# Asking for the first attention unit's keys and query at other places of the projection stage

## The chip, the cores and the metric

The kernel runs on one core of a Trainium2 chip. The metric is the device time of one execution in microseconds (us); of several runs the median is given.

## The reference

Two independent layers work on inputs of 2048 positions and 448 channels, and their outputs are joined along the last axis.

```python
# layer A: a diagonal state-space convolution
K = 2.0 * einsum("dn,dnl->dl", C, exp((A * dt[:, None])[:, :, None] * pos)).real
y = irfft(rfft(u_t, 2 * L) * rfft(K, 2 * L))[:, :, :L] ; y = y + u * D_skip
# layer B: attention with 16 heads of 28 channels
q, k, v = split(x @ wqkv)
p = softmax(einsum("bhqd,bhkd->bhqk", q, k) * scale)
b = einsum("bhqk,bhkd->bhqd", p, v) @ wo
return concatenate([a, b], axis=-1)
```

All arithmetic is float32 or close to it: the queries and keys are kept as a high and a low part, stacked in rows of 32 partitions.

## The kernel before

**Units of attention.** The 16 heads are four groups (`G`) of four heads (`HG`), the 2048 queries are four chunks of 512 (`CQ`). A unit is one group and one chunk; the units 0 to 15 are worked off in that order. For each unit three tensors lie in on-chip memory: the stacked keys `khat` of the group (one 128 x 2048 slab per head j, of four transfers of 256 KB), the stacked queries `qhat` (four transfers of 256 KB) and the key differences `kdif` of the group (for each head four transfers of 64 KB). `load_k(g, j, pool)`, `load_q(u, rows)` and `load_kd(g, j, rows)` ask for them. They are read from DRAM buffers that the projection has written (`k<-hl`, `q<-hl` and `kd<-dhl` in the profile).

**The first stage** does two things side by side until unit 0 can start. TensorE projects x into q, k and v: a list `work` of 48 jobs, for each of the four chunks c the k and q of groups 0 to 3 and four blocks of v; in the last chunk the four v blocks come first, so the last eight jobs are k0, q0, k1, q1, k2, q2, k3, q3. A job is issued by `project()`, and the evacuation of the job *before* it follows: ScalarE and VectorE write the high and low halves into a tile `hl`, which has two buffers, and one transfer of 512 KB takes it to DRAM. Beside that, `seeds(o)` for o = 0 to 7 prepares layer A on VectorE, ScalarE and GpSimd, in 13 steps each, and writes two tiles to DRAM (`sd<-sg`, step 11, and `sd<-qhat`, step 12). The second one is built in a `qhat` buffer: `places` (step 8) takes it with two GpSimd memsets. There are three `qhat` buffers, shared by the seeds and by the queries of the units.

**The order** is written out in slots t = 0 to 40. Step i of `seeds(o)` lies in slot 4o + i. In each slot the projection advances to 48(t+1)/37 jobs, then the seeds' steps follow, then what `ahead` holds for the slot:

```python
A0, A1, KW = 26, 34, (33, 35, 36)
ahead = collections.defaultdict(list)
for i in range(2 * HG):
    ahead[A0 + i].append(lambda i=i: load_kd(0, i // 2, range(2 * (i % 2), 2 * (i % 2) + 2)))
for i in range(2):
    ahead[A1 + i].append(lambda i=i: load_q(0, range(2 * i, 2 * i + 2)))
for j, t in enumerate(KW):
    ahead[t].append(lambda j=j: load_k(0, j, k0_p))
...
for t in range(n_stage):
    while work and n_work - len(work) < n_work * (t + 1) / PW:   # PW = 37
        project()
    for f in slots[t] + ahead.get(t, []):
        f()
```

After slot 36 the last evacuation, the fourth head's keys (`load_k(0, 3)`), the query of unit 1 and the v tiles of group 0 are asked for. In this stage the order of the program is a priority for the scheduler and not a fixed order (`KEPT["p"]` is empty); all transfers are issued from one engine, SyncE, whose queue (SPq) is worked in order. The slab of head j in `khat` of group 0 also holds the projection weights of group j until the last q and k of that group have been projected, so its load waits for TensorE.

**The maxima of unit 0** come behind the slots: for each of 16 pairs (head, block of 128 queries), four matmuls of 512 keys. The first uses `kdif` and goes through ScalarE (`rl`, Relu), VectorE joins it to the second, and reduces the third and the fourth (`mx`). Their end is `m<-mx`, a transposition, and the start of the attention loop, in which every engine's order is fixed.

In the profile nearly every instruction carries the line of one helper, L75, so groups are told apart by the names of the tiles.

Of the kernel before, what the change touches and what calls it, by code (L numbers as in the profile page):

```python
# [40 lines left out]
PS = 1  # L41
SGB, XB, XL = 2, 5, 4
K0, KP, KD, UP = 0, 3.5, 4, 3
A0, A1, KW = 26, 34, (33, 35, 36)

N1 = 32
N2 = 64
# [43 lines left out]
def body(ctx, tc, a, out):  # L91
# [5 lines left out]
    def pool(stack, name, bufs=1, space=None, side=None):  # L97
        kw = {} if space is None else {"space": space}
        if side:
            kw["side"] = side  # L100
        return stack.enter_context(tc.tile_pool(name=name, bufs=bufs, reuse_waits="tile", **kw))
# [31 lines left out]
    k0_p = pool(k0_st, "k0_p", side="right")  # L133
# [11 lines left out]
    def load_k(g, j, p):  # L145
        if j == 0:
            t = k0_t if g == 0 else p.tile([128, HG, L], F32R, name="khat")
            kt_g[g] = [t[:, i] for i in range(HG)]
        for r in range(4):
            nc.sync.dma_start(kt_g[g][j][32 * r:32 * r + 32, :].bitcast(F32), k_d[g][r % 2, 32 * j:32 * j + 32, :])  # L150
# [3 lines left out]
    def load_v(g, c):  # L154
        v_g[g, c] = t = v_p.tile([128, NK // NQ, HG, 32], F32, name="v", bufs=5)
        nc.sync.dma_start(t.rearrange("p t h e -> p t (h e)"), v_d[c][:, g])
# [8 lines left out]
    def load_q(u, rows=range(4)):  # L165
        g, c = divmod(u, NQ)
        if 0 in rows:
            q_u[u] = q_p.tile([128, HG, CQ], F32R, name="qhat", bufs=3)
        t = q_u[u]
        for r in rows:  # L170
            nc.sync.dma_start(t[32 * r:32 * r + 32].bitcast(F32), q_d[g][c][r // 2].rearrange("(j p) q -> p j q", j=HG))
# [40 lines left out]
    with ExitStack() as st:  # L212
# [47 lines left out]
        t = a["A_log_dt"]  # L260
# [252 lines left out]
        ahead = collections.defaultdict(list)  # L513
# [2 lines left out]
        for i in range(2):  # L516
            ahead[A1 + i].append(lambda i=i: load_q(0, range(2 * i, 2 * i + 2)))

        for j, t in enumerate(KW):
            ahead[t].append(lambda j=j: load_k(0, j, k0_p))  # L520

        def project():

            e = work.pop(0)() if work else None
            while pend:
                pend.pop(0)()
            if e:
                pend.append(e)

        for t in range(n_stage):  # L530
            while work and n_work - len(work) < n_work * (t + 1) / PW:
                project()
            for f in slots[t] + ahead.get(t, []):
                f()
            if t + 1 == PW:
                project()
                wst.close()
                load_k(0, HG - 1, k0_p)
                load_q(1)
                for c in range(NQ):  # L540
                    load_v(0, c)
# [581 lines left out]
```

## Time and profile before

| | us |
|---|---|
| median of three runs (1330.11 to 1336.95) | 1332.18 |
| the profiled execution, device time | 1331.76 |
| its span in the profile | 1329.9 |

| engine | busy us | share of the span |
|---|---|---|
| TensorE, matmul (PE) | 1235.2 | 93% |
| VectorE (DVE) | 990.1 | 74% |
| ScalarE (ACT) | 953.2 | 72% |
| GpSimd (POOL) | 838.4 | 63% |

The attention loop starts near 260 us, and from there TensorE is busy in nearly all of its time. The shares above are averages over the first stage and the loop. All times below are counted from the start of the span. The 1.9 us between the span and the device time lie outside the profile.

### The profile page before, as it was taken

To read this page: it belongs to the slowest core of one execution; us is meant where nothing else is said; L and a number is where in the kernel's file an instruction comes from. 1 tells how busy PE (TensorE), PEld (TensorE's weight loads), DVE (VectorE), ACT (ScalarE), POOL (GpSimd) and SP (SyncE) were. 2 spreads that over 40 slices of the span, in tenths; PEclk is the share of its full clock that TensorE was granted. 3 is DMA by queue.
4 is the path that set the end of the run, shared out by engine and by line. 5 is a ranking of instruction groups with operands and counts; after the bars stand their busy time and mean duration, and the time that the engine had idled before them with its cause. 6 is when DMAs were issued, how large, how long until landed. Compare 5 with 4: busy or idle time off the path is not lost.

```text
span 1329.9 us, 33195 instructions
## 1 busy us (share of the span) xinstructions
PE 1235.2 (93%) x12625; PEld 705.0 (53%) x12625; DVE 990.1 (74%) x2138; ACT 953.2 (72%) x2067; POOL 838.4 (63%) x704
## 2 busy tenths in 40 slices
PE   6878885699999999999999999999999999898997
PEld 5656763355555555555555555555555545444433
DVE  5897786787777887787788988888886858757311
ACT  4876762388888888888888888888886656555553
POOL 2686681378788788888779999989992202211211
PEclk9989888799999999999999999999999999999999
DMA  6677669725856546468634233732415553825485
GB/s 188 207 272 264 217 211 287 206 57 122 191 134 152 128 129 163 135 165 235 172 95 95 61 72 89 165 78 69 100 50 148 192 157 134 263 102 162 150 217 140
DMA packets 200088, 205.36 MB, mean 154 GB/s; under 512 B 95992, under 2 KB 158520, under 8 KB 197880
## 3 DMA queue, kind: packets, MB, share of 16 engines
q1 hardware_dynamic: 199928, 203.23, 55.1%
q8 instruction: 100, 1.64, 0.5%
q14 instruction: 60, 0.49, 0.1%
HBM read 120.73 MB, written 82.18 MB: 153 GB/s over the span
## 4 chain that ended last, share of the span: by engine, by line
PE 69%; DVE 14%; DMA 5%; ACT 5%; POOL 4%; issue 2%; SPq 1%; ACTq 0%; POOLq 0%; DVEq 0%
PE pm L75 39%; PE pss L75 15%; PE po L75 15%; DVE mx L75 2%; DVE p L75 2%; DVE tri L75 2%; DVE pr L75 1%; POOL qhat L75 1%; ACT p L75 1%; DVE rl L75 1%; DVE sg L75 1%; DVE qhat L75 1%; ACT tri L75 1%; DMA qhat<-q 1%; DVE px L75 1%
## 5 line engine op out<-in xcount | busy, mean ns | idle before, releaser
L75 ACT ACTIVATE p<-pss 128x512 f32<-128x512 f32 x1024 | 561.6, 611 | 118.7 <-PE pss L75 114.3
L75 PE MATMUL pss<-qhat,khat 128*128 128x512 f32 x1024 | 403.3, 400 | 3.8 <-ACT p L75 3.7
L75 DVE TENSOR_REDUCE mx<-pm 128x1 f32<-128x512 f32 x500 | 321.5, 684 | 102.4 <-PE pm L75 100.9
L75 PE MATMUL pm<-khat,qhat 128*128 128x512 f32 x749 | 326.9, 439 | 19.3 <-DVE mx L75 6.7
L75 POOL TENSOR_TENSOR e<-e,sdb 128x256 f32<-128x256 f32 x168 | 201.8, 1201 | 126.7 <-ACT e L75 107.8
L75 PE MATMUL po<-p,v 128*32 128x512 f32 x2048 | 269.9, 596 | 0.0
L75 POOL TENSOR_TENSOR e<-e,eu 128x256 f32<-128x256 f32 x168 | 248.1, 1477 | 13.2
L75 PEld LDWEIGHTS pm<-khat,qhat 128*128 128x128 f32 x749 | 141.5, 189 | 215.1 <-ACT p L75 47.0
L75 DVE CUSTOM_DVE_ANT_0 rl<-pm,rl 128x512 f32<-128x512 f32 x249 | 171.5, 689 | 66.0 <-ACT rl L75 62.2
L75 PEld LDWEIGHTS pss<-qhat,khat 128*128 128x128 f32 x1024 | 190.6, 188 | 50.8 <-ACT p L75 12.4
L75 POOL TENSOR_TENSOR eu<-e,sdb 128x256 f32<-128x256 f32 x168 | 202.0, 1202 | 0.0
L75 POOL TENSOR_TENSOR p<-pr,pr 64x448 f32<-64x448 f32 x32 | 40.9, 1278 | 197.3 <-DVE pr L75 186.3
L75 DVE TENSOR_TENSOR g<-g,zg 128x128 f32<-128x128 f32 x392 | 162.1, 414 | 4.0 <-ACT zg L75 0.6
L75 ACT ACTIVATE rl<-pm 128x512 f32<-128x512 f32 x249 | 151.1, 607 | 16.8 <-PE pm L75 16.8
L75 PE MATMUL pm<-xh,khat 112*128 112x512 f32 x256 | 92.3, 444 | 21.3 <-DVE hl L75 9.8
L75 PE MATMUL pm<-kdif,qhat 128*128 128x512 f32 x249 | 100.9, 405 | 2.3 <-DVE mx L75 1.3
L75 DVE TENSOR_TENSOR zg<-g,zg 128x128 f32<-128x128 f32 x224 | 87.9, 392 | 5.1
L75 PEld LDWEIGHTS pm<-e,g 128*32 128x32 f32 x3584 | 57.6, 110 | 44.0 <-issue 17.8
L75 PE MATMUL pm<-e,g 128*32 128x64 f32 x3584 | 73.7, 222 | 1.9 <-POOL e L75 1.9
L75 ACT ACTIVATE y<-pm 128x448 f32<-128x448 f32 x48 | 26.3, 549 | 65.9 <-issue 32.8
L75 PEld LDWEIGHTS pm<-xh,khat 112*128 112x128 f32 x256 | 53.4, 213 | 36.6 <-DVE hl L75 11.2
L75 PEld LDWEIGHTS po<-p,v 128*32 128x32 f32 x2048 | 55.8, 110 | 22.4 <-issue 17.9
(134 smaller groups left out, 1503.9 us busy)
## 6 DMA issues: line engine op xcount, KB each, us to landing
sdb<-sd SPq DMA_DIRECT2D x56, 336.0 KB
khat<-k SPq DMA_DIRECT2D x64, 256.0 KB
qhat<-q SPq DMA_DIRECT2D x64, 256.0 KB
sd<-sg SPq DMA_DIRECT2D x8, 1456.0 KB
k<-hl SPq DMA_DIRECT2D x16, 512.0 KB
q<-hl SPq DMA_DIRECT2D x16, 512.0 KB
mw<-in_mw SPq DMA_DIRECT2D x16, 512.0 KB
sd<-qhat SPq DMA_DIRECT2D x8, 896.0 KB
```

What stands on the lines that cost most here:

```text
L75: i = f(*args, **kw)
```

## The change

The eight requests for parts of `kdif` move from the slots 26 to 33 to the slots 16 to 23. The two requests for the halves of the first query `qhat` move from the slots 34 and 35 to 24 and 25. The keys of heads 0, 1 and 2 keep their slots 33, 35 and 36, but stand at the head of the slot, before its projection and its seeds' steps; until now they stood at its end. Nothing is computed differently, and the number of instructions and transfers stays the same.

```diff
-A0, A1, KW = 26, 34, (33, 35, 36)
+A0, A1, KW = 16, 24, (33, 35, 36)
...
-        for j, t in enumerate(KW):
-            ahead[t].append(lambda j=j: load_k(0, j, k0_p))
+        firsts = {t: lambda j=j: load_k(0, j, k0_p) for j, t in enumerate(KW)}
...
         for t in range(n_stage):
+            if t in firsts:
+                firsts[t]()
             while work and n_work - len(work) < n_work * (t + 1) / PW:
                 project()
             for f in slots[t] + ahead.get(t, []):
```

## Prediction

> **What bounds the kernel now.** I read the page first, for the size of the stage that the change touches.
>
> ```profile
> PE   6878885699999999999999999999999999898997
> ```
>
> One digit is 33 us. From the ninth on TensorE is at 9 nearly throughout: that is the attention loop, which the change does not enter. What it can save or lose lies in the first eight digits and shifts all that follows. In them I read the chain that ended last, to find where the stage passes from projection to attention.
>
> ```profile
> 203.16 11.80 DMA qhat<-q
> 214.96 0.14 issue
> 215.10 0.78 PE pt L75
> 215.90 0.61 ACT rl L75
> 216.53 0.69 DVE rl L75
> ...
> 247.47 0.21 DVE m L75
> ```
>
> The columns are start, duration and what ran. For 11.8 us the chain is one transfer, the second half of unit 0's query; the maxima begin when it has landed. On VectorE they last from 216.53 to 247.47, 30.9 us. Next I read the timelines of SyncE's queue, ScalarE, VectorE and TensorE around that wait, to see what is late once the query is not.
>
> ```profile
> 184.39 1.24 SPq L75 DMA_DIRECT2D sd<-qhat  x1
> 185.68 2.55 SPq L75 DMA_DIRECT2D kdif<-kd  x2
> 188.33 1.20 SPq L75 DMA_DIRECT2D k<-hl  x1
> 194.90 0.38 SPq L75 DMA_DIRECT2D q<-hl  x1
> 195.32 1.32 SPq L75 DMA_DIRECT2D kdif<-kd  x2
> 196.75 1.75 SPq L75 DMA_DIRECT2D khat<-k  x4
> 198.96 0.39 SPq L75 DMA_DIRECT2D k<-hl  x1
> 199.40 1.69 SPq L75 DMA_DIRECT2D qhat<-q  x2
> 201.19 0.42 SPq L75 DMA_DIRECT2D q<-hl  x1
> 201.65 0.58 SPq L75 DMA_DIRECT2D sd<-sg  x1
> ```
>
> ```profile
> 205.16 0.69 ACT L75 ACTIVATE hl<-pm,kones 128x512 fp32r<-128x512 f32 x1 [6.68 <-DMA k<-hl]
> ```
>
> ```profile
> 205.88 0.75 DVE L75 SCALAR_TENSOR_TENSOR hl<-pm,kones,hl 128x512 fp32r<-128x512 f32 x1 [4.26 <-ACT hl L75]
> ...
> 210.94 0.69 DVE L75 TENSOR_TENSOR hl<-pm,hl 128x512 fp32r<-128x512 f32 x1 [1.05 <-ACT hl L75]
> ```
>
> ```profile
> 203.21 0.40 PE L75 MATMUL pm<-xl,khat 112*128 112x512 f32 x1
> ```
>
> Four things are to be seen. In this stretch SyncE's queue stands in the order of the program: slot 33 gives k<-hl (188.33, job k1) and q<-hl (194.90, q1), then its requests; slot 34 k2 (198.96), slot 35 q2 (201.19). TensorE ends the last projection, q3, near 203.6 and then waits. The evacuation of k3 (ScalarE 205.16) waits 6.68 us for k2's transfer, whose buffer it takes: issued at 198.96, that lands near 205.1, 6.2 us later, behind the first head's four key transfers of 196.75. And VectorE finishes the last evacuation, q3, at 211.63 (210.94 + 0.69), so today's wait for the query hides a second one that ends only 4.9 us before 216.53.
>
> **The change, part by part.** The sizes that pass through the queue:
>
> ```profile
> khat<-k SPq DMA_DIRECT2D x64, 256.0 KB
> sd<-sg SPq DMA_DIRECT2D x8, 1456.0 KB
> k<-hl SPq DMA_DIRECT2D x16, 512.0 KB
> ...
> sd<-qhat SPq DMA_DIRECT2D x8, 896.0 KB
> ```
>
> ```profile
> 120.00:125.00 5.00, 5.00 (x27) 3.84 (x27) 3.32 (x5) 1.66 (x3) 2.25 (x1) 1.00 1.05 385
> 190.00:195.00 5.00, 2.33 (x11) 1.58 (x9) 3.88 (x6) 4.06 (x6) 2.76 (x2) 0.94 0.48 176
> 200.00:205.00 5.00, 3.61 (x13) 2.54 (x12) 1.51 (x5) 0.00 (x0) 4.40 (x5) 0.88 0.97 263
> ```
>
> The last two columns are the DMA engines' busy share and GB/s: full engines move 0.26 (200 to 205) to 0.38 MB per us (120 to 125); I take 0.30, nearer the row of this stretch.
>
> *The query leaves.* Four transfers, two at 199.40 and two behind the sd<-sg of 201.65, go to the slots 24 and 25. The 11.8 us wait goes entirely. Next late is the evacuation chain above, not TensorE.
>
> *The first head's keys rise* in the queue from 196.75 to about 186, behind sd<-qhat and ahead of k1 (188.33). They need k0's transfer and q0's matmuls, both past. Their 1.05 MB need 3.5 us; between 190 and 195 the engines were half idle (0.48), and the kdif pairs that stood here are gone, so k1 and q1, which follow, land in time for their buffers. Cost: nothing; without that cover, up to 3.5 us on the evacuation of k2, which takes k1's buffer.
>
> *k2's transfer* then has no keys ahead of it. Its time lies between 6.2 us (as now) and that of a transfer with an empty queue; the nearest row for the latter is q1's on the chain:
>
> ```profile
> 194.90 2.87 DMA q<-hl
> ```
>
> I take 2.9, because the keys of head 1 stand behind k2 (slot 35) and no longer head 0's ahead of it. It lands near 201.9 instead of 205.1, and k3's evacuation on ScalarE and VectorE runs 3.2 us sooner. The Trainium skill, page DMA: Bandwidth & Descriptors, section Anatomy of one DMA, fits a transfer at about 2.0 us plus its bytes at 436 GB/s, on the GpSimd path; for 512 KB that estimates 3.2 us, and the sum below would be 1325.1. It is measured on another issuing path, so the row of this case stands.
>
> *q3's evacuation* follows on VectorE behind the seeds' steps (205.88 to 210.94), so by VectorE's order it ends 3.2 us sooner, at 208.4. It also needs q2's buffer. In the new order the four key transfers of head 1 stand ahead of q2: 1.57 MB in all after k2's landing at 201.9, at 0.30 MB per us 5.2 us, so 207.1. ScalarE's half of q3 comes some 0.6 us before VectorE's, so it is wanted at 210.94 − 3.2 − 0.6 = 207.1 as well. At 0.26 MB per us it is 207.9, 0.8 us more. sd<-sg stands behind q2, as now.
>
> *The maxima* then begin when VectorE is through with q3, at about 208.5 rather than 216.53: **−8.0 us**. Query, kdif and head 0 are there, and TensorE and ScalarE have no more than 1.4 us to do (215.10 to 216.53), which lies before 208.5. Their 30.9 us stay, if the other heads arrive in time. A head is used up in a quarter, 7.7 us. Behind q2 come sd<-sg (1.5 MB) and head 2 (1.05 MB, before k3 now): 2.5 MB or 8.5 us, so near 215.6, needed at 208.5 + 15.5 = 224. Head 3 has k3, sd<-qhat and q3 (about 2 MB) and itself ahead, 10 us more, so 226, needed at 231.7. Both hold, with 5 us to spare in the worse case.
>
> *The kdif and query requests among earlier work.* They pass SyncE's queue ahead of evacuations, seeds' writes and x loads some ten slots earlier. The dear place is where the chain is a transfer while the engines are full (120 to 125, 1.05):
>
> ```profile
> 119.78 6.49 DMA k<-hl
> ```
>
> All of kdif (sixteen transfers of 64 KB, 1.05 MB) would cost 2.7 us there at 385 GB/s; the two slots that really fall there, four times 64 KB, 0.7 us. A gain of as much is possible where they are gone (the kdif rows of 185.68 and 195.32 are the last of them), though q1 there waits for VectorE and not for the queue. Between −2.7 and 2.7 I take **+0.7**.
>
> *A qhat buffer is taken ten slots longer.* The query now holds one of three from slot 24 on, so the seeds of o = 6 must build in the buffer that sd<-qhat of o = 4 frees, and not that of o = 3.
>
> ```profile
> 164.20 3.50 POOL L75 TENSOR_TENSOR qhat<-qhat 128x336 f32<-128x336 f32 x1 [0.88 <-DVE tri L75]
> ...
> 180.17 1.43 POOL L75 TENSOR_TENSOR qhat<-qhat 128x336 f32<-128x336 f32 x1 [0.97 <-DVE qhat L75]
> ...
> 196.35 0.53 POOL L75 MEMSET qhat<- 128x112 f32 x2
> ```
>
> ```profile
> 163.42 0.57 SPq L75 DMA_DIRECT2D sd<-qhat  x1
> ```
>
> These are the first products of o = 5 and of o = 6, and the memsets of o = 7. The new buffer comes free when the write issued at 163.42 lands, by an estimate 6 us later (its 0.9 MB and the like of the 1.5 MB that sd<-sg queued before it, at 0.30): 169.4. If the memsets of o = 6 are queued behind the products of o = 5, that is past and costs nothing; if ahead of them, GpSimd stands from 164.20 to 169.4, 5.2 us, with those products behind it, and VectorE waits for them. A gain is excluded, since a buffer only becomes scarcer. I take **+0.3**, near the lower end: o = 7 has the same spacing today, and its memsets stand late in the queue (196.35).
>
> **Sum.** −8.0 + 0.7 + 0.3 = −7.0 against the profiled execution, 1331.76: **1324.8 us**. Its time is 0.4 below the median of 1332.18. About 0.5% (6.7 us) is what a measurement of this kernel can tell from no change.
>
> **The rivals.**
>
> *Half of it (1328).* The list order is a priority only, and SyncE stands from 189.5 to 194.90 waiting for VectorE's q1: if head 0's keys stay behind it, or head 1's slip ahead of k2 in their place, k2 still lands near 205 and the maxima start right after 211.63: −4.9 + 1.0, 1327.9. For it: the wait of ScalarE is for buffers, and the same megabytes still pass in this stretch. Against: the queue follows the program's order in every row above.
>
> *GpSimd waits for the buffers (slower, 1340).* Should the memsets of o = 6 be queued early, they cost 5.2 us; and if those of o = 7 are moved likewise, ahead of o = 6's products (180.17), they wait for the write issued at 184.39 to land, near 190.4, 10.2 us more. Together 15.4 on an engine on which VectorE's chain depends: 1331.8 − 8.0 + 0.7 + 15.4 = 1339.9. It decides from the point where such a write lands after the memsets' turn; up to 7 us of wait the change still comes out even. For it:
>
> ```profile
> 125.08 0.56 POOL L75 MEMSET qhat<- 128x112 f32 x2 [0.91 <-DMA sd<-qhat]
> ```
>
> This wait exists already for another o, with a buffer to spare. Against: it was 0.91 us.
>
> *More than that (1321).* The queue loses twenty requests between 150 and 204, and the evacuations there run sooner too; 2.7 us of kdif's bytes and the 1.0 of costs not paid give 1331.8 − 8.0 − 2.7, about 1321.
>
> **How the numbers follow.** The main case has 0.48, the half 0.22, the waiting GpSimd 0.25, the larger gain 0.05. GpSimd has that much because every reordering of this stage is free to move the memsets, and the buffer does become scarcer. The main case runs from 1322 to 1328, and a little over six tenths of it, 0.30, lie below 1325.5, where 0.5% begins; with the larger gain that makes 0.35 for faster. Same: 0.18 + 0.22 = 0.40. Slower: 0.25. The range holds the main case, the half, most of the larger gain and the smaller waits on GpSimd (one of 5 to 10 us, with the half of the gain): 1319.5 to 1337.
>
> **What would show it.** Right: no wait of TensorE for qhat<-q; four khat<-k near 186 ahead of k1's k<-hl; ScalarE's wait for k<-hl before k3's evacuation down from 6.68 to about 3.5 us; the first rl on VectorE near 208.5 and m<-mx near 239.5; and the loop the same but shifted. Wrong: khat<-k still behind 194.9, VectorE's q3 evacuation still near 211, GpSimd waiting several us for sd<-qhat, or a stretch before 185 that is longer than now. If everything up to 203 shifts by several us, the scheduler has ordered the stage anew and my sum has left that out.

## The result, and the profile after

The changed kernel takes 1348.15 us, the median of six runs (1341.90 to 1352.73), against 1331.14 for six runs of the kernel before: a ratio of 1.0114 with a 95% interval of 1.0091 to 1.0136. It is slower by 1.1%; forecast were 1324.8 us and a range up to 1337. The profiled execution took 1349.5 us, 17.7 more than that of before.

The row of TensorE in the page of the changed kernel, one digit for each 34 us, answers to the first line of the prediction:

```profile
PE   6878767799999999999999999999999999898998
```

The fifth and the sixth digit fall (8 and 8 before, now 7 and 6); the seventh and the eighth rise (5 and 6 before, now 7 and 7), because projections now run there. So the time went in the first stage, ahead of the loop, and largely ahead of the stretch that the prediction worked on. The chain that ended last shows where (start, duration, what ran):

```profile
177.36 4.85 PE pm L75 x12
183.75 10.80 PE pm L75 x36
195.56 2.25 POOL tri L75
...
226.51 6.19 DMA q<-hl
```

The 11.8 us for qhat<-q are gone, as forecast. In their place stand projections, at an hour when the chain of before was long past most of them, and GpSimd's work for the last seeds. The same rows as in the prediction, first ScalarE's evacuation of k3, then VectorE's first `rl`, its evacuation of q3 and the end of the maxima, then TensorE's last projection, each from its engine's timeline:

```profile
227.94 0.69 ACT L75 ACTIVATE hl<-pm,kones 128x512 fp32r<-128x512 f32 x1 [4.76 <-DMA k<-hl]
```

```profile
221.55 0.68 DVE L75 CUSTOM_DVE_ANT_0 rl<-pt,rl 128x512 f32<-128x512 f32 x1
...
233.43 0.69 DVE L75 TENSOR_TENSOR hl<-pm,hl 128x512 fp32r<-128x512 f32 x1 [0.46 <-ACT hl L75]
...
262.00 0.20 DVE L75 TENSOR_REDUCE m<-mx 128x16 f32<-128x48 f32 x1
```

```profile
228.39 0.40 PE L75 MATMUL pm<-xl,khat 112*128 112x512 f32 x1
```

The last projection comes 25 us later than before (203.21), the end of the maxima 14.5 us later (247.47). The first `rl` stands alone ahead of that: the next one comes at 235.50, when q3's evacuation is done. From there the loop runs nearly as before, shifted by 14.9 us at its start and 17.8 at its end. What happened ahead of 200 us is read from SyncE's queue. First three rows of before, which the prediction had not shown, then the changed kernel:

```profile
140.37 0.83 SPq L75 DMA_DIRECT2D nat<-in_A_log_A_real  x1
...
147.58 0.37 SPq L75 DMA_DIRECT2D k<-hl  x1
...
156.63 0.62 SPq L75 DMA_DIRECT2D sd<-sg  x1
```

```profile
97.87 1.54 SPq L75 DMA_DIRECT2D kdif<-kd  x2
...
112.42 0.87 SPq L75 DMA_DIRECT2D nat<-in_A_log_A_real  x1
...
156.54 2.29 SPq L75 DMA_DIRECT2D qhat<-q  x2
158.87 1.24 SPq L75 DMA_DIRECT2D v<-vst  x1
160.16 1.67 SPq L75 DMA_DIRECT2D qhat<-q  x2
161.87 15.98 SPq L75 DMA_DIRECT2D v<-vst  x2
177.95 0.87 SPq L75 DMA_DIRECT2D nat<-in_A_log_A_real  x1
...
184.32 0.63 SPq L75 DMA_DIRECT2D sd<-sg  x1
...
203.90 4.39 SPq L75 DMA_DIRECT2D khat<-k  x4
208.40 0.38 SPq L75 DMA_DIRECT2D k<-hl  x1
```

`nat` is the input of the seeds. For the last of them (o = 7) it was asked for at 140.37, ahead of its slot: its slot is 26, and the k<-hl of 147.58 behind it (k3 of the third chunk) belongs to slot 23. Now it stands behind two writes of the v blocks, which wait 16 us for ScalarE's evacuation, and comes at 177.95. The delay starts earlier than that. The first kdif requests stand at 97.87, where `nat` of o = 5 stood before (97.17); that one now comes at 112.42, and that of o = 6 at 143.51 and no longer at 122.75. The write sd<-sg of o = 4 slides from 156.63 to 184.32 for the same reason. Three engines wait for what hangs on this (the bracket is the wait ahead of the row, and what ended it):

```profile
192.07 0.93 DVE L75 TENSOR_TENSOR sg<-tri 128x336 f32<-128x336 f32 x2 [15.74 <-DMA sd<-sg]
```

```profile
195.56 2.25 POOL L75 TENSOR_TENSOR tri<-tr,pw 128x1232 f32<-128x1232 f32 x1 [16.31 <-ACT tr L75]
```

```profile
177.36 0.74 PE L75 MATMUL pm<-vh,xh 112*128 112x448 f32 x1 [13.74 <-ACT vst L75]
...
180.88 0.57 PE L75 MATMUL pm<-vh,xh 112*128 112x448 f32 x1
183.75 0.74 PE L75 MATMUL pm<-vh,xh 112*128 112x448 f32 x1 [1.12 <-ACT vst L75]
...
189.51 0.57 PE L75 MATMUL pm<-vh,xh 112*128 112x448 f32 x1
...
190.14 0.37 PE L75 MATMUL pm<-vh,xl 112*128 112x448 f32 x1
```

VectorE stands because `sg` has two buffers (`SGB`), and the one it needs is given free by the late write. TensorE stands because ScalarE evacuates the v block only behind a row of the seeds' steps, which wait themselves:

```profile
171.07 1.23 ACT L75 ACTIVATE tri<-tri 128x1232 f32<-128x1232 f32 x1 [3.13 <-DVE tri L75]
...
176.37 0.57 ACT L75 ACTIVATE sg<-px 128x112 f32<-128x112 f32 x2 [0.48 <-DVE sg L75]
176.73 0.58 ACT L75 ACTIVATE vst<-pm 128x448 f32<-128x448 f32 x1
```

The table by stretches (start and end, length, busy time of PE, PEld, DVE, ACT and POOL, granted TensorE clock, DMA share, GB/s), before and then after:

```profile
170.00:180.00 10.00, 7.53 (x35) 5.78 (x34) 8.42 (x17) 6.97 (x19) 8.46 (x12) 0.86 0.18 50
180.00:190.00 10.00, 10.00 (x37) 7.92 (x36) 10.00 (x18) 4.99 (x7) 9.68 (x7) 0.79 1.02 355
```

```profile
170.00:180.00 10.00, 2.64 (x7) 2.38 (x8) 6.12 (x11) 5.37 (x9) 8.23 (x8) 0.50 0.10 31
180.00:190.00 10.00, 8.88 (x24) 7.30 (x24) 0.00 (x0) 5.30 (x10) 0.00 (x0) 0.50 0.58 193
```

Between 180 and 190 VectorE and GpSimd, full before, do nothing at all. And TensorE pays twice: the granted clock falls to 0.50, and a matmul of the v projection takes 0.57 us at 180.88, against 0.37 at 190.14, where the clock is back.

### The profile page after: what moved, and what is told of

The parts are those of the page before. It is cut to its first block, busy times and chain, and to the rows that moved or that the text cites. A ratio compares the mean times of both kernels' runs of the same rounds, so it can differ in the third digit from the quotient of the medians.

```text
span 1347.7 us, 33201 instructions
## 1 busy us (share of the span) xinstructions
PE 1245.7 (92%) x12625; PEld 711.3 (53%) x12625; DVE 988.0 (73%) x2138; ACT 956.7 (71%) x2069; POOL 838.0 (62%) x704
## 4 chain that ended last, share of the span: by engine, by line
PE 71%; DVE 13%; POOL 5%; ACT 4%; DMA 4%; issue 3%; SPq 1%; ACTq 0%; POOLq 0%; DVEq 0%
PE pm L75 41%; PE po L75 15%; PE pss L75 15%; DVE mx L75 2%; POOL qhat L75 2%; DVE p L75 2%; DVE pr L75 1%; DVE tri L75 1%; ACT p L75 1%; DVE rl L75 1%; DVE px L75 1%; DMA sdb<-sd 1%; DVE sg L75 1%; DMA khat<-k 1%; DVE qhat L75 1%
```

## The experiments

Theory: the moved requests cost their turns in SyncE's in-order queue, and thereby the turns of the requests on which the seeds wait. Rivals: the bytes among earlier work; the `qhat` buffer that the query holds ten slots longer; the keys ahead of k1. All ratios are to runs of the kernel before on the same chip, with their 95% intervals.

**Each part by itself.** The key differences alone:

```diff
-A0, A1, KW = 26, 34, (33, 35, 36)
+A0, A1, KW = 16, 34, (33, 35, 36)
```

> Only the kdif requests move, to the slots 16 to 23; query and keys stay as before the change. Queue theory (requests that are always ready take the turns in SyncE's queue in which the seeds' inputs, nat, and the writes sd<-qhat stood ahead of their slot, so that the last nat is queued behind v<-vst writes that wait for ScalarE): the last nat later than 165 us instead of 140, and the time 8 to 18 us above before. Buffer theory (the query holds a qhat buffer and the seeds wait for one): no query has moved, so within 3 us of before. Keys theory (the keys at the head of their slots hold up the evacuations behind them): within 3 us of before.

Measured: 1337.30 us, 1.0027 (1.0007 to 1.0047). That is some 4 us, and not the 8 to 18 of the queue theory: it had the direction and not the size.

The query alone:

```diff
-A0, A1, KW = 26, 34, (33, 35, 36)
+A0, A1, KW = 26, 24, (33, 35, 36)
```

> Only the two query requests move, to the slots 24 and 25. Queue theory: four requests can push one nat group back, so the loss is smaller than with kdif: from 5 us faster (the wait of 11.8 us for the query is gone, the evacuation of q3 ends 4.9 us before) to 8 us slower. Buffer theory: the whole loss is here, 12 to 20 us slower than before, and GpSimd's memsets for o = 5 or 6 stand tens of us later than before, with a wait for sd<-qhat. Keys theory: about 5 us faster.

Measured: 1337.48 us, 1.0035 (1.0016 to 1.0054). This is within the queue theory's range and far below the 12 to 20 us of the buffer theory. The last `nat` in SyncE's queue, in the kernel with kdif alone and in that with the query alone:

```profile
159.72 1.38 SPq L75 DMA_DIRECT2D nat<-in_A_log_A_real  x1
```

```profile
160.12 0.87 SPq L75 DMA_DIRECT2D nat<-in_A_log_A_real  x1
```

Either part pushes it back by 20 us, both together by 38 (177.95). With the query GpSimd also waits for a buffer, as the rival said:

```profile
201.23 0.51 POOL L75 MEMSET qhat<- 128x112 f32 x2 [3.23 <-DMA sd<-qhat]
```

The keys alone, with A0 and A1 as before:

```diff
-            ahead[t].append(lambda j=j: load_k(0, j, k0_p))
+        firsts = {t: lambda j=j: load_k(0, j, k0_p) for j, t in enumerate(KW)}
```

> Only the keys of heads 0 to 2 move to the head of their slots. Queue and buffer theory: nothing before 185 us changes; head 0's keys are issued near 186 ahead of k1, the evacuation of k3 waits less, but the query's second half still stands behind sd<-sg, so 0 to 5 us faster. Keys theory: the loss is here, 8 us or more slower, with ScalarE's waits for k<-hl and q<-hl longer than before.

Measured: 1339.58 us, 1.0055 (1.0035 to 1.0075), and in a second series 1336.30, 1.0032 (1.0014 to 1.0050): slower, as the keys theory said, but by 4 to 7 us and not by 8 or more. The last `nat` stays at 140.29 here. SyncE's queue, then ScalarE's evacuation of k2, then the stretch of 190 to 195:

```profile
187.43 2.61 SPq L75 DMA_DIRECT2D khat<-k  x4
190.15 0.38 SPq L75 DMA_DIRECT2D k<-hl  x1
```

```profile
198.43 0.69 ACT L75 ACTIVATE hl<-pm,kones 128x512 fp32r<-128x512 f32 x1 [2.64 <-DMA k<-hl]
```

```profile
190.00:195.00 5.00, 1.49 (x5) 0.86 (x5) 3.44 (x6) 5.00 (x10) 2.34 (x3) 0.72 1.03 229
```

This is the order that the prediction wanted, head 0's keys ahead of k1, and it costs: the engines, half idle there before (0.48), are full (1.03), and k2's evacuation waits 2.64 us for k1's transfer. The first `rl` comes at 218.40, 1.9 us later than before. Together the three parts make 0.27 + 0.35 + 0.55 = 1.17%, with the second series of the keys 0.94%; the whole change makes 1.14%. With intervals of 0.2% on each part this does not show that the parts simply add up.

> The kernel that only sets the keys at the head of their slots, once more, for a second profile. If the 6 us that its loop lost near 610 us (ScalarE waiting for sdb<-sd) belong to the order of the program, this profile shows them again and the ratio is 1.0055 again; if they fell on that one execution, the loop is shifted by about 2 us throughout and the profiled span is near 1332.

Both profiles of this kernel lose another 6 us in the loop: near 611 and 627 us ScalarE waits for sdb<-sd, 5.7 us in the first and 5.4 in the second, in before 0.39. The timed runs of the second series go from 1332.43 to 1341.82, so the waits seem not to be the same in each. What sets them stays open.

**Giving the seeds their turns back.** The whole change, with the request for `nat` three slots sooner:

```diff
-                slots[max(SP * o + (i or -2), 0)] += st_
+                slots[max(SP * o + (i or -5), 0)] += st_
```

> The whole change, and the seeds' input step (four nat transfers) is listed three slots sooner (step 0 in slot 4o - 5 instead of 4o - 2), which puts it ahead of most of the moved kdif requests in the order of priority. Queue theory: the last nat is issued near 150 us, and more than half of the loss of 17 us is recovered: 1340 or less. Buffer theory and keys theory: neither buffers nor keys are touched, so the time stays at 1345 to 1351.

Measured: 1338.60 us, 1.0051 (1.0030 to 1.0072). Somewhat more than half of the loss is back (1.0114 before this edit). SyncE's queue and VectorE's wait:

```profile
150.01 1.28 SPq L75 DMA_DIRECT2D nat<-in_A_log_A_real  x1
```

```profile
185.51 0.93 DVE L75 TENSOR_TENSOR sg<-tri 128x336 f32<-128x336 f32 x2 [7.08 <-DMA sd<-sg]
```

What is left has a part of the buffer in it: in this kernel GpSimd's memsets wait 6.39 us at 162.19 and 6.89 us at 191.61 for sd<-qhat. The same edit on the kernel before, as a control, and on that with the query alone:

> Control: the kernel before with the seeds' inputs listed three slots sooner and nothing else. Queue theory: its inputs were in time already, so within 4 us of before; if it gains much, the recovery seen with the whole change is not the return of a loss but a gain of its own.

> Only the query moves, to the slots 24 and 25, and the seeds' inputs are listed three slots sooner, so that the last nat keeps its place ahead of the v<-vst writes. Queue theory: the loss of the query's move (4.7 us) came from that nat, so this is faster than the query alone, and with the query's wait gone at least level with the same kernel without the query's move (the next run). Buffer theory: GpSimd's memsets still wait for sd<-qhat (3.2 us where the query alone was moved), and 3 us or more of the loss stay.

Measured: 1330.48 us, 0.9988 (0.9975 to 1.0001), and 1335.29 us, 1.0023 (1.0007 to 1.0038). So an earlier `nat` by itself is no change that can be measured, and in the changed kernel it is worth 0.6%: it mends something that the change broke. With the query alone it brings the last `nat` back to 141.14, but at most a third of the loss (the two intervals overlap). The queue theory had asked for more, and the buffer theory's 3 us are still there. GpSimd's wait for the buffer is longer than without the edit; but TensorE, too, waits 5.26 us for ScalarE's `vst` at 172.53, so that the buffer is not shown to be all that remains. GpSimd's wait, from its timeline:

```profile
199.99 0.56 POOL L75 MEMSET qhat<- 128x112 f32 x2 [7.51 <-DMA sd<-qhat]
```

**Another queue.** The test that decides: the whole change, slots and all, but its ten requests are issued from GpSimd and no longer from SyncE.

```diff
-    ahead[A0 + i].append(lambda i=i: load_kd(0, i // 2, range(2 * (i % 2), 2 * (i % 2) + 2)))
+    ahead[A0 + i].append(lambda i=i: load_kd(0, i // 2, range(2 * (i % 2), 2 * (i % 2) + 2), nc.gpsimd))
...
-    ahead[A1 + i].append(lambda i=i: load_q(0, range(2 * i, 2 * i + 2)))
+    ahead[A1 + i].append(lambda i=i: load_q(0, range(2 * i, 2 * i + 2), nc.gpsimd))
```

> The whole change, slots and all, but the ten moved requests (kdif, first query) are issued from GpSimd's queue instead of SyncE's. Theory (they cost because they take turns in SyncE's in-order queue from requests on which the seeds wait): the last seeds' inputs are asked for near 141 us again and not at 178, VectorE no longer waits 15.7 us for sd<-sg, and most of the 16 us go away; 1333 to 1338 us, what is left being the early keys (6 to 7 us by the run that moved only them) less the query's wait (some 5), plus the turns of 24 requests on GpSimd. Rival (it is the qhat buffer that the query holds ten slots longer, and the bytes among earlier work): both are here as in the whole change, so 1345 or more, with GpSimd waiting for sd<-qhat.

Measured: 1328.84 us, 0.9970 (0.9958 to 0.9981). Not only the loss is gone, the kernel is faster than before, and below my own theory's 1333 to 1338. (The requests are twenty transfers, and not the 24 that the expectation names.) SyncE's queue, then GpSimd's, then VectorE's first `rl`:

```profile
141.23 0.82 SPq L75 DMA_DIRECT2D nat<-in_A_log_A_real  x1
```

```profile
75.42 0.66 POOL L75 DMA_DIRECT2D kdif<-kd  x1
...
126.23 1.14 POOL L75 DMA_DIRECT2D qhat<-q  x2 [0.56 <-DMA sd<-qhat]
...
174.86 0.55 POOL L75 MEMSET qhat<- 128x112 f32 x2 [2.03 <-DMA sd<-qhat]
```

```profile
202.80 0.68 DVE L75 CUSTOM_DVE_ANT_0 rl<-pt,rl 128x512 f32<-128x512 f32 x1
```

The query takes its buffer at 126.23, thirty us sooner than in the changed kernel (156.54), and kdif's bytes pass still earlier (from 75.42, and not from 97.87). The buffer is held even longer, the bytes pass among earlier work, the keys stand ahead of k1, and this costs 2.03 and 0.56 us of GpSimd's waiting and 5.09 us of ScalarE's, ahead of k3's evacuation; the last `nat` is 0.9 us later than before. The bytes do not pass in the same stretch as in the changed kernel, so their price there is not measured. Its control has the slots of before and issues from GpSimd, and the third kernel has the sooner slots without the keys' part:

> The slots of the kernel before, but the ten requests for kdif and the first query are issued from GpSimd's queue. If the gain of the same with the changed slots (1328.8, 0.997) comes only from taking 24 requests off SyncE, this is as fast: 1328 to 1329.5. If the sooner slots add to it, this is slower by what they add: the query is then asked for among GpSimd's later work, and the kernel lies between 1329.5 and 1333.

> The changed slots of kdif and query, issued from GpSimd, with the keys at the end of their slots as before. Theory (the keys at the head of their slots put a megabyte ahead of k1 in a stretch whose engines are full, and k2's and k3's evacuations wait for it): without that the first maxima come sooner than 202.8 and the kernel takes 1324 to 1327 us. Rival (with the query out of the stretch the keys do no harm, since the maxima now start on head 0's keys): 1328.5 to 1331, head 0's keys come later and the maxima wait for them.

Measured: 1328.37 us, 0.9972 (0.9960 to 0.9984), and 1325.92 us, 0.9958 (0.9943 to 0.9973). The last is the fastest kernel of the study. Its time is the expected one, but the sign that was to go with it is not there: the first `rl` comes at 208.66, later than 202.80, and only from the second on (214.30 against 216.84) is it ahead. With GpSimd issuing, the whole change is worth nothing (0.9970 against 0.9972); through SyncE it costs 1.1%. In the control kdif goes as early as here (from 76.17), so that of the slots only the query's and the keys' are tested; its query is issued from 172.99 on, and that too is early enough. The keys' part still seems to cost, 0.9970 with it and 0.9958 without, but the intervals overlap. The end of the maxima with and without it, from VectorE's timelines:

```profile
243.35 0.20 DVE L75 TENSOR_REDUCE m<-mx 128x16 f32<-128x48 f32 x1
```

```profile
241.86 0.20 DVE L75 TENSOR_REDUCE m<-mx 128x16 f32<-128x48 f32 x1
```

**What the query's wait was worth.** Two slots sooner (32 instead of 34) the query passes none of the requests for `nat`; alone, and with the keys' part, which is the order that my sum reckoned with:

```diff
-A0, A1, KW = 26, 34, (33, 35, 36)
+A0, A1, KW = 26, 32, (33, 35, 36)
```

> The kernel before, with only the two query requests at slots 32 and 33 instead of 34 and 35: SyncE's queue keeps its order up to the write sd<-qhat near 184 us, and the query stands ahead of sd<-sg. My sum of the transition (query wait gone, evacuation of q3 next, which ends 4.9 us before the maxima start): 4 to 6 us faster. Rival (the transfers of this stretch are bound by bytes, so the wait only goes over to the first head's keys): within 2 us of before, with a wait for khat<-k of some 10 us where the wait for qhat<-q stood.

> As the previous one, and the keys of heads 0 to 2 at the head of their slots. This is the order of transfers that my prediction reckoned with, without the far moves. My sum of the transition: 8 us faster, about 1325. Rival (the engines are bound by bytes here, so the keys that pass k1 delay its landing and with it the evacuation of k2, as they did where the keys alone were moved): 0 to 8 us slower than before, with ScalarE's wait for k<-hl ahead of k2's evacuation 2 us or more.

Measured: 1330.61 us, 0.9993 (0.9979 to 1.0007), and 1334.24 us, 1.0016 (1.0003 to 1.0029). The query alone is no change that can be measured, where 4 to 6 us were expected; with the keys' part it is slightly slower, where 8 us faster were expected. From the VectorE timeline of the query alone the first `rl` and the end of the maxima, and from its chain what took the query's place:

```profile
210.89 0.69 DVE L75 CUSTOM_DVE_ANT_0 rl<-pt,rl 128x512 f32<-128x512 f32 x1 [6.04 <-PE pm L75]
...
244.62 0.20 DVE L75 TENSOR_REDUCE m<-mx 128x16 f32<-128x48 f32 x1
```

```profile
216.95 11.32 DMA khat<-k
```

The maxima begin 5.6 us sooner and end 2.85 sooner: head 2's keys are late next. But the stage itself was no longer that of before. ScalarE now evacuates k2 behind copies of the seeds (`sg`), at 202.81 where it was 196.63, and TensorE waits for that; first these two rows, then the end of the maxima with the keys' part:

```profile
202.81 0.65 ACT L75 ACTIVATE hl<-pm,kones 128x512 fp32r<-128x512 f32 x1
```

```profile
204.30 1.22 PE L75 MATMUL pm<-xh,khat 112*128 112x512 f32 x2 [7.09 <-DVE hl L75]
```

```profile
249.02 0.20 DVE L75 TENSOR_REDUCE m<-mx 128x16 f32<-128x48 f32 x1
```

TensorE's last projection so comes at 209.16 and not at 203.21. With the keys' part the order is the same: k2's evacuation at 206.03, the last projection at 211.87, VectorE's evacuation of q3 not done before 221.0, where my sum had 208.4, and the maxima end 1.55 us later than before. Head 2's keys are in time there, and ScalarE's wait for k<-hl ahead of k2's evacuation, which the rival named, is absent. A move of two slots is thus enough to change ScalarE's order, with the last `nat` at 140.07 as before.

Then, from the query alone, that stretch's 1.5 MB of sd<-sg (o = 6), asked for three slots later, behind the keys:

```diff
+                slots[max(SP * o + (i or -2), 0) + (3 if (o, i) == (6, 11) else 0)] += st_
```

> The query two slots sooner (32), and the 1.5 MB of sd<-sg of seeds(6) asked for three slots later, behind the keys. Theory (from 180 to 240 us the stretch is bound by bytes, so whichever transfer leaves makes the next one early): head 2's keys land about 5 us sooner than the 228.3 of the kernel with the query alone, and m<-mx comes at 240.5 to 242.5 instead of 244.6; 1327 to 1329 us. Rival (after the query is out of the way, the evacuations of k3 and q3 on ScalarE and VectorE set the maxima): the same as with the query alone, 1330.6 us, m<-mx near 244.6.

Measured: 1333.79 us, 1.0005 (0.9991 to 1.0019); m<-mx at 245.49. Neither number of the theory came, though TensorE's wait for head 2's keys is gone. In this execution the stage ran 3 us later already at the last projection (212.16 against 209.16). Counted from there, the maxima end after 33.3 us and not 35.5; but the loop's first exponentials then wait 11.2 us and not 8.7 for sdb<-sd. The transfer left one queue of waiters and joined the next. This is read from one profile of each and not more than an indication.

## Why the prediction was wrong

**The step that failed** is the reading that "in this stretch SyncE's queue stands in the order of the program", carried over to the slots 16 to 25, and with it the term "the kdif and query requests among earlier work", +0.7 us. I had priced the bytes of these requests and not their turns. Ahead of 180 us the queue of before does not stand in the program's order: the last `nat` (slot 26, at 140.37) goes ahead of a write of slot 23 (147.58). The moved requests take such turns (kdif from 97.87 on, the query at 156.54 and 160.16), and `nat` and sd<-sg fall behind writes that wait for ScalarE. The price is that of the whole result: 1.0114 through SyncE, 0.9970 with the same slots through GpSimd. What the bytes cost by themselves is not measured; with kdif and query on GpSimd, where they pass at another time, the last `nat` is 0.9 us later than before. The last sentence of the prediction named this case and gave it neither price nor chance.

**The query leaves, −8.0 us.** This term failed too, without any help from `nat`. The wait did go, and in the changed kernel the evacuation of q3 was next, as said. But the sum kept every evacuation and projection at its place. With the query two slots sooner and the keys at the head of their slots, which is the order that it reckoned with, k2's evacuation went behind seeds' work, the last projection came at 211.87 and not at 203.21, q3's evacuation ended at 221.0 and not at 208.4, and the kernel was no faster (1.0016). And the sum took the 30.9 us of the maxima as fixed "if the other heads arrive in time": with the query alone at slot 32, where head 2's keys stand behind k3 and not ahead of it, they landed at 228.3 (216.95 + 11.32), and of the 5.6 us at the start of the maxima 2.85 were left at their end. In no kernel did the maxima end 8 us sooner; the nearest was 5.6 (241.86), with kdif and query on GpSimd.

**The first head's keys, "cost: nothing".** Wrong: 0.32 to 0.55% alone. The half-idle engines between 190 and 195 were not spare: k1's transfer passes there, now landed 8.2 us after its request, and k2's evacuation waited for it. So the cover failed, and the cost lay within the 3.5 us that I had allowed "without that cover"; the stage lost 1.9 us at the first `rl` in one profile, and what that profile lost beyond it lies in the loop. In the changed kernel the keys did go ahead of k1, at 203.90 and not near 186, and ScalarE's wait ahead of k3's evacuation went from 6.68 to 4.76 us, not to 3.5.

**The buffer, +0.3.** The rival's mechanism exists: waits on GpSimd of 3.23 us and 7.51 us with the query alone at slot 24 through SyncE, of 6.39 and 6.89 in the changed kernel with `nat` listed sooner, of 2.03 and 0.56 through GpSimd's queue. In the changed kernel itself GpSimd's long wait (16.31 us) is for ScalarE's `tr`, made from the late `nat`. Of the rivals "GpSimd waits for the buffers" came out nearest in time (1340), but not by its cause.

**Open:** ScalarE's order changed as well, with the evacuation of the v blocks behind seeds' work, which made the 16 us wait in the queue. The runs do not tell whether that follows from the queue's order or was chosen beside it. Both vanish together when the requests leave SyncE; but with the query at slot 32 ScalarE's order changed while the last `nat` kept its place, so a change beside the queue is possible. That kdif and query on GpSimd would race ahead to 75 and 126 us, and cost nothing there, I had not foreseen either.

## What to carry to other kernels

A request that is moved sooner in an in-order queue costs the requests behind it, not only its bytes: list what is queued between its old and its new place, and look there for the one that the longest chain of later work hangs on. Where program order is only a priority, check in the trace, at the place where the request will land, whether the queue really stands in that order; a stretch elsewhere proves nothing. A reordering can also reach engines whose work was not touched, as ScalarE's evacuations show: a sum that keeps all other work at its place needs a price for that. If the queue is the trouble, another engine's queue may take the requests: here that turned +1.1% into −0.3%, and without the moved keys into −0.4%; but the unmoved slots gave −0.3% on that queue as well, so that the gain is not shown to come from the move.

## What the runs showed of the hardware

Two things I had not expected. Around TensorE's wait of 13.74 us the granted clock was 0.50 from 170 to 190, and the matmuls of 448 columns that followed it took 0.57 us until then and 0.37 from 190.14 on, so that a stall in this stage cost more than its length. The Trainium skill, page TensorE: Matmul & The Clock Gate, Part 1, says that an idle array runs at half its clock and comes back some 4 us into sustained work; the trace agrees on the half, but here it took from 183.75, the end of the last short wait, to 190.14, 6.4 us. And twenty transfers issued from GpSimd among its own arithmetic cost it little: 0.5 to 0.66 us each (0.66 for the first, 2.00 for four), with no loss that the total shows.
